# Attention inside an attention, expert and feed-forward kernel: maxima nine steps ahead of the scores instead of ten, the splits of v one step later

## The chip, the core and the metric

One core of a Trainium2 chip runs the whole program. TensorE (PE; its weight loads PEld) multiplies, VectorE (DVE), ScalarE (ACT) and GpSimd (POOL) do the element work, and SyncE (SP) issues nearly all transfers, in the order of the program. The metric is the device time of one execution in microseconds (us). Before the change the median of three runs is 687.61 us (685.89 to 688.62).

## The reference, cut to what matters

```python
# attention: q, k, v are (2, 8, 768, 64); proj is (64, 6)
q_bits = einsum(q, proj) > 0 ; k_bits = einsum(k, proj) > 0
q_bucket = sum(q_bits * 2**i) ; k_bucket = sum(k_bits * 2**i)
scores = where(q_bucket == k_bucket, 1/8 * q @ k.T, -1e9)
scores = scores - max(scores)            # over the keys
attn = exp(scores) / (sum(exp(scores)) + 1e-9)
x = (attn @ v) as (1536, 512)
# router and experts: 8 experts, each token goes to one of them
logits = x @ w_gate + modality_bias[modality_id]
e = argmax(logits) ; gate = softmax(logits)[e]
x = gate * (relu(x @ w1[e]) @ w2[e])
# feed-forward
h = x @ w_in
out = (max(h, 0) + alpha * min(h, 0)) @ w_out
```

Queries and keys match where all six signs of their projections agree. The kernel computes this match as matrix products of rows of signs (the hash), so that the mask comes out of the same multiplication as the scores.

## The kernel before

The program runs the attention first (to about 242 us), then the experts, then the feed-forward layers. The change touches the attention alone, with the router operations that are laid between its steps. There are 16 heads and 96 steps: step s computes the scores of head s // 6 for the key block s % 6 against all 768 queries.

The loop over s (L950 to L975) writes the work of a step in the order of a string of letters (ORDER), and every engine runs its instructions in the order in which they are written. A step holds:

- a and b: ST, the scores of two halves of 384 queries, two matmuls each (L861, L862), and ScalarE's exponential (L863). The matmul L861 reads rows of the head's operand tile `op`: its signs and, in row 96, the row `mr`, minus the maxima of the queries.
- m and n: MAX, the products of signs (L829) for a key block u that lies some steps ahead, and VectorE's maxima over them (L830). How far ahead is set by LA: u stays below s + 6 + LA + 1. The tuple cap limits how many blocks the first steps take.
- e: the 16-bit copy of the exponentials and what it leaves (L867 on ScalarE, L868 on GpSimd).
- p: POSTa, the maxima of a head put together when its sixth block is done (L832). One step later, at the step's end, POSTb transposes them on TensorE (L835), VectorE makes the row from that (L837), and SyncE writes it into the operand tile (L838); two flag rows (L841, L842) follow a step later.
- A: AV, the products with v (L876 to L878) of two steps at a time, in odd steps.
- N: NORM, the normalisation of a head that is done (L888 to L890).
- V and o: the work that the table PLAN sets to a step: vsplit, ScalarE's scaling of a head's v (L755, in V) and VectorE's split in two parts (L759, L760, in o).
- L, last in the step: what PLAN sets there, in the order in which it was registered: T (the split of a head's q and k: L711, L712, and five transfers of operand rows, L650), Z (the hash matmuls L802 to L804 of a half of 384 columns, VectorE's comparison L809, and four transfers of hash rows), vtot (12 small matmuls with v's sums, L766 to L769), vscale and vscale2 (L734 to L749), POSTb.
- D: the transfers that the step before put off: hash rows first, then operand rows and flag rows, then loads of later heads (L656, L657).

Score and maxima products share five PSUM tiles, and everything small that TensorE writes shares two, called misc. After each step the function hook runs: the router's constants, transpositions and logits of x, and the router's first lumps (the list first: each entry is the step in which the generator goes one lump further). The lumps that the change moves are the token positions (L346 to L353), the one-hot table (L357, L274) and the gates (L233 to L239). In steps 80 and 81 the hook issues the first expert's weight loads (L630).

PLAN's entries for a group are added to its first step: sp gives the step of vsplit of each of four heads in a period of 24 steps, tot how many steps later its vtot runs, Z3 the steps of head 3's two hash halves.

Of the kernel before, what the change touches and what calls it, by code (L numbers as in the profile page):

```python
# [22 lines left out]
G = 2  # L23
NP = 5
NH = 16
LA = 4
MO3 = "HMTh"
STEPS = 13.0
DELAY = 0.7
# [8 lines left out]
ORDER = "aVDNmbnefopAL"  # L38
PM = 2
PLAN = dict(  # L40
    v0=(1, 3, 4), T3=(2, 2), Z3=(4, 5), T=(2, 4, 5, 7), Z=(8, 10), ld=0, am1=(4, 6, 8, 9), am=(4, 6, 8,
    10), sc=(13, 15), tot=3, tot0=6, sp=(-2, 4, 10, 18), cap=(3, 2, 0, 1), x=(1, 2, 7, 3), x3=(0, 1, 2, 2), x4=(9, 10, 13, 11), w1=(91, 92, 95, 96, 97, 98, 99, 100), ga=(87, 88, 90), vl=1, am0=(0, 0), Z2=(0, 1), x6=(0, 1, 6, 4), first=(57, 58, 59, 60, 66, 72, 75, 78, 83, 84, 85, 86),
)
NPRE = 3
NT = 22
# [458 lines left out]
def _program(base, tc, nc, q, k, v, proj, mod, w_gate, mbias, w1, w2, win, wout, alpha, out):  # L504
# [445 lines left out]
    for s in range(96+LAG+2):  # L950
        us=[u for u in range(nu,min(96,s+6+LA+1,nu+(PLAN["cap"][s] if s<len(PLAN["cap"]) else 2)))]; nu+=len(us)
        fs=dq[:]; dq.clear()
# [615 lines left out]
```

## Time and profile before

| | |
|---|---|
| median of three runs | 687.61 us |
| profiled execution, as a run | 686.88 us |
| its span, first to last instruction | 685.1 us |
| PE busy | 656.4 us (96%) |
| PEld busy | 556.2 us (81%) |
| DVE busy | 446.7 us (65%) |
| ACT busy | 315.3 us (46%) |
| POOL busy | 236.0 us (34%) |
| mean granted TensorE clock | 0.987 of 2.4 GHz |

The span is one execution; the 1.8 us that it lacks to the run's time lie around it. A busy TensorE counts overlapping matmuls as one stretch, so a share of 96% does not say that nothing waits: a wait shows as an idle time before an instruction, with what ended it. The attention is where other engines are busy too; the last 443 us are long chains of matmuls.

### The profile page before, as it was taken

What the parts mean: (1) busy time and instruction counts of PE and PEld (TensorE: products, weight loads), DVE (VectorE), ACT (ScalarE), POOL (GpSimd) and SP (SyncE); (2) the same over time, 40 slices, a digit from 0 to 9 for tenths busy, and PEclk for the clock granted to TensorE, in tenths of its full rate; (3) what the DMA queues carried; (4) which work ended last, traced back from release to release, by engine and by line L of the source; (5) the groups of instructions that cost most, each with busy time, mean ns of one, the idle gap of its engine ahead of it and who ended that gap; (6) DMA issues with size and microseconds to landing.
All of it is one profiled execution on the core that took longest, in us unless ns stands there. A gap on an engine that the chain in (4) does not pass through costs nothing.

```text
span 685.1 us, 12778 instructions
## 1 busy us (share of the span) xinstructions
PE 656.4 (96%) x4938; PEld 556.2 (81%) x4938; DVE 446.7 (65%) x927; ACT 315.3 (46%) x536; POOL 236.0 (34%) x211
## 2 busy tenths in 40 slices
PE   7789999999999988999999999999999999999995
PEld 6578898998788878898888987888888888888884
DVE  6887878788888778455735668999443444433332
ACT  5567788887787843033423256665211111111111
POOL 8767999987967501310000202040030000200002
PEclk9979999999999999999999999999999999999998
DMA  8466864866603139385320834441020000100001
GB/s 217 129 146 142 187 154 97 185 185 138 140 11 125 49 107 395 119 321 201 108 61 11 285 120 154 131 146 62 1 93 1 15 16 0 47 16 0 1 0 61
DMA packets 32859, 75.02 MB, mean 110 GB/s; under 512 B 7276, under 2 KB 7366, under 8 KB 32534
## 3 DMA queue, kind: packets, MB, share of 16 engines
q1 hardware_dynamic: 29700, 64.43, 33.0%
q0 software_dynamic: 2960, 9.70, 4.3%
q8 instruction: 39, 0.64, 0.4%
q14 instruction: 30, 0.25, 0.1%
q10 hardware_dynamic: 130, 0.00, 0.0%
HBM read 49.79 MB, written 14.68 MB: 94 GB/s over the span
## 4 chain that ended last, share of the span: by engine, by line
PE 54%; DVE 1%; ACT 1%; issue 1%; POOL 1%; ACTq 0%; POOLq 0%
PE o L1413 19%; PE h L1387 18%; PE y L1074 8%; PE g L1054 8%; PE tr L1257 1%; POOL out_dram L1430 1%; PE tr L1041 0%; DVE w L1232 0%; DVE op L1232 0%; ACT op L1230 0%; DVE gl L620 0%; ACT gf L1391 0%; ACT q L1392 0%; ACT w L1230 0%; DVE big L1197 0%
## 5 line engine op out<-in xcount | busy, mean ns | idle before, releaser
L868 POOL TENSOR_TENSOR El<-E,Eh 128x768 f16<-128x768 f32 x87 | 142.7, 1652 | 36.6 <-ACT Eh L867 22.7
L863 ACT ACTIVATE E<-st 128x384 f32<-128x384 f32 x192 | 89.2, 494 | 53.3 <-PE st L862 49.8
L830 DVE TENSOR_REDUCE mx<-mxp 128x1 f32<-128x384 f32 x192 | 97.6, 548 | 9.2 <-PE mxp L829 8.7
L617 ACT ACTIVATE gh<-gf 128x512 fp32r<-128x512 f32 x48 | 30.3, 631 | 142.7 <-PE o L1413 132.2
L867 ACT ACTIVATE Eh<-E 128x768 f16<-128x768 f32 x94 | 79.8, 849 | 0.0
L861 PE MATMUL st<-op 97*128 97x384 f32 x192 | 72.9, 380 | 1.6 <-DMA op<-mr 1.3
L829 PE MATMUL mxp<-op 76*128 76x384 f32 x192 | 65.9, 357 | 7.3 <-ACT E L863 2.5
L620 DVE TENSOR_TENSOR gl<-gf,gh 128x512 fp32r<-128x512 f32 x48 | 33.1, 690 | 59.2 <-ACT gh L617 57.2
L1430 POOL DMA_INDIRECT out_dram<-x,did x12 | 11.8, 984 | 167.8 <-DVE x L1427 89.1
L1387 PE MATMUL h<-big,op 128*128 128x512 f32 x256 | 67.9, 393 | 0.0
L862 PE MATMUL st<-op 128*128 128x384 f32 x192 | 65.8, 343 | 0.0
L1413 PE MATMUL o<-op,gh 128*128 128x512 f32 x192 | 64.2, 395 | 0.0
L1245 POOL DMA_INDIRECT yg<-ys,dpos x10 | 12.3, 1231 | 138.3 <-DVE x L1197 72.8
L876 PE MATMUL av<-vh,Eh 128*128 128x65 f16 x576 | 58.5, 196 | 1.3 <-DVE big L890 1.3
L876 PEld LDWEIGHTS <-Eh 128*128 128x128 f16 x576 | 52.5, 98 | 8.4 <-issue 6.2
L1074 PE MATMUL y<-op,hh 128*128 128x512 f32 x172 | 58.6, 399 | 0.0
L877 PE MATMUL av<-vl,Eh 128*128 128x64 f16 x576 | 58.0, 194 | 0.0
L878 PE MATMUL av<-vh,El 128*128 128x65 f16 x576 | 57.8, 195 | 0.0
L1387 PEld LDWEIGHTS h<-big,op 128*128 128x128 f32 x256 | 48.1, 188 | 10.9
L877 PEld LDWEIGHTS <-Eh 128*128 128x128 f16 x576 | 53.2, 99 | 0.0
L878 PEld LDWEIGHTS <-El 128*128 128x128 f16 x576 | 53.1, 98 | 0.0
L1395 DVE TENSOR_SCALAR gf<-h,al 128x512 f32<-128x512 f32 x33 | 24.8, 751 | 41.7 <-PE h L1387 41.7
(424 smaller groups left out, 1483.2 us busy)
## 6 DMA issues: line engine op xcount, KB each, us to landing
r<-in_moe_w_dram SPq DMA_DIRECT2D x14, 1024.0 KB
op<-B SPq DMA_DIRECT2D x32, 192.0 KB
op<-A SPq DMA_DIRECT2D x28, 192.0 KB
op<-A SPq DMA_DIRECT2D x13, 384.0 KB
ys<-zero SPq DMA_DIRECT2D x19, 256.0 KB
op<-in_moe_w_in_dram SPq DMA_DIRECT2D x4, 1024.0 KB
op<-in_moe_w_out_dram SPq DMA_DIRECT2D x4, 1024.0 KB
ys<-ysb SPq DMA_DIRECT2D x13, 256.0 KB
```

The costliest lines, as they stand in the source:

```text
L829: mm(p[:,0:384],t[0:76,2,c*128:(c+1)*128],t[0:76,1,a*384:a*384+384],start=True,stop=True)
L830: nc.vector.tensor_reduce(out=mx[h][:,c,a:a+1],in_=p[:,0:384],axis=AX.X,op=ALU.max)
L861: mm(p[:,0:384],t[0:97,1,js],t[0:97,2,qs],start=True,stop=False)
L863: nc.scalar.activation(E[s][0][:,qs],p[:,0:384],AF.Exp,scale=0.125)
L867: else: nc.scalar.activation(eh,e,AF.Copy)
L868: (nc.vector if s>=ELD else nc.gpsimd).tensor_tensor(out=el,in0=e,in1=eh,op=ALU.subtract)
L876: mm(a[:,c*65:c*65+65],eh[:,cs],VH[h//4%2][:,j,h%4,:],start=(j==0 and c==0),stop=False,skip_group_check=True)
L877: mm(a[:,c*65:c*65+64],eh[:,cs],VL[h//4%2][:,j,h%4,:],start=False,stop=False,skip_group_check=True)
L878: mm(a[:,c*65:c*65+65],el[:,cs],VH[h//4%2][:,j,h%4,:],start=False,stop=False,skip_group_check=True)
L1074: nc.tensor.matmul(yps[key][i], a[:, ts], w[:, c], start=(c == 0 and m == 0), stop=(c == 7 and m == 2))
L1387: nc.tensor.matmul(p, terms[t][0][:, kk, cs], terms[t][1][:, kk], start=(n == 0), stop=(n == 11))
L1413: nc.tensor.matmul(po[b][i], a[:, ts], w[:, c % 2], start=(c == 0 and n == 0), stop=(c == 15 and n == 2))
```

## The change

Six entries of the tables change. No instruction is added or taken away; the order changes.

```diff
-LA = 4
+LA = 3
 ...
-    Z3=(4, 5), ... tot=3, ... sp=(-2, 4, 10, 18), cap=(3, 2, 0, 1),
+    Z3=(5, 5), ... tot=2, ... sp=(-1, 5, 11, 17), cap=(3, 2, 0, 1, 0),
 ...
-    first=(57, 58, 59, 60, 66, 72, 75, 78, 83, 84, 85, 86),
+    first=(57, 58, 59, 60, 66, 72, 78, 80, 81, 84, 85, 86),
```

With LA = 3 a step's maxima are those of the block nine steps on instead of ten, and so POSTa and POSTb of a head come one step later: POSTb of head h moves from the end of step 6h - 4 to the end of step 6h - 3. Head 1's stay in steps 3 and 4, since the limits of the first four steps are the same. Step 4 has no maxima. The splits of three heads of four come a step later and of the fourth a step earlier, all now in the step behind a NORM; vtot of the three stays, of the fourth it comes two steps earlier. Head 3's first hash half moves from step 4 to step 5, and the router's lumps move: positions from step 75 to 78, one-hot table from 78 to 80, gates from 83 to 81.

On TensorE, head 5's transposition L835 stood at the end of an even step, behind two score pairs and two maxima (op_143 is head 4's operand tile, whose scores these are; mt_182 the maxima of odd heads):

```order
 L861 MATMUL st<-op_143 128x384
 L862 MATMUL st<-op_143 128x384
-L829 MATMUL mxp<-op_140 128x384
+L829 MATMUL mxp<-op_139 128x384
 L861 MATMUL st<-op_143 128x384
 L862 MATMUL st<-op_143 128x384
-L829 MATMUL mxp<-op_140 128x384
-L835 MATMUL misc<-ident,mt_182 6x128
+L829 MATMUL mxp<-op_139 128x384
```

It now stands behind the odd step's products with v (av; the last two are the flag rows fl and v's sums vt):

```order
 L882 LDWEIGHTS fl_187
 L882 MATMUL av<-vt,fl_187 128x65
+L835 MATMUL misc<-ident,mt_182 6x128
 L861 MATMUL st<-op_143 128x384
 L862 MATMUL st<-op_143 128x384
```

So L835 moved behind the 36 products of two steps, and the maxima of the step are those of the block before.

On SyncE the order around it stays. This is the queue from head 5's row (op_139) to head 6's (op_140), the same before and now; A and B are the two parts of the q and k of heads 8 and 9, big_74 holds the loaded q and k:

```order
66 L838 DMA op_139<-mr 1x6x128
67 L842 DMA fl_189<-ft 1x6x128 x2
68 L650 DMA op_142<-A 64x2x768
69 L650 DMA op_142<-A 64x768 x2
70 L650 DMA op_142<-B 64x768 x2
...
76 L656 DMA big_74<-in_k_dram 64x768
77 L657 DMA big_74<-in_q_dram 64x768
78 L838 DMA op_140<-mr 1x6x128
```

Nothing moved in this piece; what changed is when its first row's data is made.

On VectorE, at the end of the piece around a NORM (L888 to L890; am are v's magnitudes, big_74 the hash rows, vh and vl the split of v):

```order
 L889 RECIPROCAL r<-r 128x6
 L890 TENSOR_TENSOR big_72<-av,r 128x6x64
+L830 TENSOR_REDUCE mx<-mxp 128x1 x2
+L731 TENSOR_REDUCE am<-vr 128x1
+L809 TENSOR_SCALAR big_74<-misc,tv 48x384
 L830 TENSOR_REDUCE mx<-mxp 128x1 x2
 L759 CAST vh_191<-misc 128x6x64
 L760 TENSOR_TENSOR vl_193<-misc,vh_191 128x6x64
-L731 TENSOR_REDUCE am<-vr 128x1
-L809 TENSOR_SCALAR big_74<-misc,tv 48x384
-L830 TENSOR_REDUCE mx<-mxp 128x1 x2
```

The split moved behind the hash comparison and two more maxima, away from the normalisation.

## Rows read from the trace of the kernel before

**Rows 1.** Windows: us, busy time of each engine (instructions), TensorE's clock, DMA share, GB/s.

```profile
32.20:42.40 10.20, 8.56 (x51) 6.79 (x51) 7.43 (x18) 4.80 (x9) 7.15 (x5) 0.50 0.53 121
94.00:109.50 15.50, 15.50 (x194) 13.72 (x193) 13.89 (x34) 12.75 (x25) 15.50 (x16) 1.00 0.93 203
```

**Rows 2.** Timeline of TensorE, steps 3 to 15: start, us, instruction, [idle before, its releaser].

```profile
31.98 0.40 PE L747 MATMUL misc<-dg,one 128*128 128x4 f32 x2 [1.54 <-DVE dg L743]
33.88 0.66 PE L829 MATMUL mxp<-op 76*128 76x384 f32 x1 [0.66 <-ACT E L863]
38.08 0.37 PE L835 MATMUL misc<-ident,mt 128*6 128x128 f32 x1 [0.98 <-DVE vl L760]
48.28 0.41 PE L829 MATMUL mxp<-op 76*128 76x384 f32 x1 [0.83 <-ACT A L711]
...
52.80 0.34 PE L861 MATMUL st<-op 97*128 97x384 f32 x1
63.09 0.41 PE L829 MATMUL mxp<-op 76*128 76x384 f32 x1 [1.26 <-DMA op<-big]
64.33 0.34 PE L829 MATMUL mxp<-op 76*128 76x384 f32 x1
```

**Rows 3.** Timeline of SyncE's queue, rows of heads 2 to 9 and their neighbours.

```profile
51.89 0.77 SPq L838 DMA_DIRECT2D op<-mr  x1
65.50 0.77 SPq L838 DMA_DIRECT2D op<-mr  x1
66.32 0.43 SPq L76 DMA_DIRECT2D mi<-in_moe_modality_id_dram  x1
80.61 0.76 SPq L838 DMA_DIRECT2D op<-mr  x1
91.65 0.72 SPq L838 DMA_DIRECT2D op<-mr  x1
118.62 0.71 SPq L838 DMA_DIRECT2D op<-mr  x1
144.07 0.92 SPq L838 DMA_DIRECT2D op<-mr  x1
146.94 0.35 SPq L892 DMA_DIRECT2D x_d<-big  x1
```

**Rows 4.** Timeline of TensorE, first score matmuls of steps and one transposition.

```profile
66.77 0.43 PE L861 MATMUL st<-op 97*128 97x384 f32 x1
85.85 0.45 PE L861 MATMUL st<-op 97*128 97x384 f32 x1 [0.71 <-DMA op<-mr]
90.69 0.27 PE L835 MATMUL misc<-ident,mt 128*6 128x128 f32 x1
93.34 0.44 PE L861 MATMUL st<-op 97*128 97x384 f32 x1
111.83 0.42 PE L861 MATMUL st<-op 97*128 97x384 f32 x1
120.00 0.42 PE L861 MATMUL st<-op 97*128 97x384 f32 x1
138.28 0.43 PE L861 MATMUL st<-op 97*128 97x384 f32 x1
145.76 0.44 PE L861 MATMUL st<-op 97*128 97x384 f32 x1
165.77 0.41 PE L861 MATMUL st<-op 97*128 97x384 f32 x1 [0.54 <-DMA op<-mr]
```

**Rows 5.** DMA busy tenths in 40 slices of 80.5:85.5, 105:110 and 132:137.

```profile
DMA  9999899989995999989999999969788280100010
DMA  9696996989959693969899799998949597592010
DMA  7989989999998979995997999999995969772201
```

**Rows 6.** Waits of TensorE from 166 to 225: us in total, times, longest.

```profile
PE mxp L829 <- ACT E L863: 1.4, 3, 0.5
```

More of the change, by code (lines that the diff above doesn't have):

```diff
@@ L40 @@
 PLAN = dict(
-    v0=(1, 3, 4), T3=(2, 2), Z3=(4, 5), T=(2, 4, 5, 7), Z=(8, 10), ld=0, am1=(4, 6, 8, 9), am=(4, 6, 8,
-    10), sc=(13, 15), tot=3, tot0=6, sp=(-2, 4, 10, 18), cap=(3, 2, 0, 1), x=(1, 2, 7, 3), x3=(0, 1, 2, 2), x4=(9, 10, 13, 11), w1=(91, 92, 95, 96, 97, 98, 99, 100), ga=(87, 88, 90), vl=1, am0=(0, 0), Z2=(0, 1), x6=(0, 1, 6, 4), first=(57, 58, 59, 60, 66, 72, 75, 78, 83, 84, 85, 86),
+    v0=(1, 3, 4), T3=(2, 2), Z3=(5, 5), T=(2, 4, 5, 7), Z=(8, 10), ld=0, am1=(4, 6, 8, 9), am=(4, 6, 8,
+    10), sc=(13, 15), tot=2, tot0=6, sp=(-1, 5, 11, 17), cap=(3, 2, 0, 1, 0), x=(1, 2, 7, 3), x3=(0, 1, 2, 2), x4=(9, 10, 13, 11), w1=(91, 92, 95, 96, 97, 98, 99, 100), ga=(87, 88, 90), vl=1, am0=(0, 0), Z2=(0, 1), x6=(0, 1, 6, 4), first=(57, 58, 59, 60, 66, 72, 78, 80, 81, 84, 85, 86),
 )
```

## The prediction, before the run

> **What bounds the kernel now.** I read the page first: TensorE is busy nearly the whole span, and the chain of waits is TensorE work almost alone, so an edit that changes no instruction, as this one, can only move stretches in which TensorE waits. Next I read the windows, to see where the clock is not full, and then TensorE's timeline through the attention (22 to 242 us): 96 steps, each two score pairs (L861, L862) and two maxima (L829), an odd step with the value products L876 to L878 of two steps at its end. The reader is to see three kinds of wait in it.
>
> First, the start. TensorE waits 1.54 us until 31.98, then runs at half clock from 32.2 to 42.4, with waits of 0.66 us (a maximum of head 2), 0.98 us (the transposition L835 of head 1, for a misc buffer that head 0's v split holds) and 0.83 us (head 3's first maximum) in steps 4 to 8 [rows 1, 2]. Second, hashes: 1.26 us until 63.09, when head 4's first maximum has its hash rows [rows 2]. Third, the maxima's row mr, which the first score pair of a head multiplies with: the pairs of heads 4 and 10 wait 0.71 and 0.54 us for it [rows 4].
>
> Then I read SyncE's queue, which explains the third. Every transfer of the attention is issued there in order. After an odd head's mr come its two flag rows, the five operand rows of one head, two loads, the same for another head, two loads, and only then the next even head's mr. From head 5's mr at 91.65 [rows 3] to 109.5 us the queues move data at a DMA share of 0.93 [rows 1]; the digits of the DMA view stay at 9 or near it until about 109.4 us, and for head 8's row until 136.4 [rows 5]. So an even head's row cannot land before the data ahead of it has, and all that data stands behind the odd head's row, whose issue TensorE's own progress sets. That loop (odd step, odd mr, 15 us of transfers, even mr, even head's first pair) is what I price.
>
> **The change, part by part.** Times are sums against the profiled execution (686.88 us with its edges, 685.1 us of span); the median of the runs shown is 687.61, 0.73 above it, and I put the sum on that.
>
> *Steps 4 to 8.* Step 4 has no maxima now and head 3's first hash half goes to step 5. The 0.66 goes, since that maximum runs a step later. The 0.98 goes, since no hash half takes a misc buffer between the v split and L835, which now gets the other one. The 0.83 goes, since head 3's first maximum runs in step 9. That is 2.47 us. A pair of maxima not yet done at this place is worth another 0.35 (two matmuls that overlap, of 0.34 to 0.41 each [rows 2]), which is paid back when the maxima end. The 1.54 stands ahead of everything that moves and stays, and so does the fall of the clock behind it. Whether the half clock ends sooner no row shows: at its earliest a third of the 10.2 us goes, worth about 1.5 us (an estimate: half of 3.4, less the waits in it); or new waits for score buffers take back 1.2 (four maxima fewer in step 4 are four more behind the split on VectorE). I take 3.0 for the gain by step 9, between 1.5 and 4.5.
>
> *Head 4's hash.* Its four issues stand behind head 2's mr, head 5's operands and two flag rows. From that mr's issue at 51.89 [rows 3] to the maximum at 63.09 [rows 2] are 11.2 us of queue. In the changed kernel the mr leaves 0.96 us (the distance of L835 at 90.69 [rows 4] and its issue at 91.65 [rows 3]) after the end of step 9, not of step 8: at 52.80 + 0.96, so the hash is there at 64.96, less the gain. The maximum that needs it stands a step later, where 64.33 is now [rows 2]. So the wait does not go although it has a step more: 0.63 of the gain is lost there.
>
> *Head 4's mr row.* Head 3's row was issued at 65.50 [rows 3], and 20.35 us later, at 85.85 [rows 4], head 4's first pair began. Now head 3's row is ready 0.96 after the end of step 15, 66.77 + 0.96 = 67.73, less the gain so far; one router issue of 0.43 (mi) goes ahead of it instead of behind [rows 3], so 67.73 + 19.9 = 87.6 less the gain: 1.7 lost, and TensorE waits some 2.4 us there instead of 0.71. Of the 3.0 so far 0.7 is left. Bounds: 2.2 gained to 0.8 lost, as the start turns out.
>
> *Heads 6, 8 and 10.* L835 of every head moves from the end of an even step to the end of the odd step behind it, which holds the value products: for head 5 from 90.69 to 93.34 [rows 4]. The pair that needs the row does not move. For odd heads I take no wait, since no data stands ahead of their rows in the queue; the rows of before, where none of them waits, bound this at a few tenths each, 2 us in all. For the even ones the loop counts:
> - Head 6: head 5's row goes 2.65 us later (94.3 against 91.65), and the data with it. The DMA digits fall at 84.7 and the pair of head 4 starts 1.15 us later [rows 4, 5]; by the same 1.15 head 6's row is there at 110.55, with 1.3 us to spare against the pair at 111.83. New wait 1.35, or 1.0 if a hole of 0.4 us in the queue closes. I take 1.2.
> - Head 8: head 7's row goes at 120.00 + 0.96, not 118.62: 2.33 later. To spare: 138.28 less 137.55, or 0.7. New wait 1.6 (1.3 to 2.2).
> - Head 10: 145.76 + 0.96 = 146.7 against 144.07, 2.65 later, of which 0.4 was idle ahead of the write of x_d at 146.94 (the row and two flag rows end there at 146.5). Nothing to spare: the pair at 165.77 waits already [rows 3, 4]. New wait 2.3 on top (2.2 to 2.65).
>
> Together 5.1. Nothing hides it: TensorE is in order, and the score pair has everything of its head behind it. Head 12 has spare time, because heads 14 and 15 have no loads behind theirs, and head 14's row, which now stands behind the first weight load of 1 MB, does not wait for it: that load has nothing left to wait for and is issued some 10 us earlier.
>
> The ring order is also what the Trainium skill says: in "DMA: Bandwidth & Descriptors", section on queues, rings and completion order, each DMA engine takes descriptors in the order of the ring. The same page puts the fixed cost of a DMA near 2.0 us (section on the anatomy of one DMA, fitted on the GpSimd path). By that price alone a row would be there 2 us after its issue whatever stands ahead, and heads 6 and 8 would not wait (the second rival's case). The trace is against it where it shows: head 4's row was issued at 80.61 [rows 3], and its pair waited until 85.85 [rows 4].
>
> *v's splits, lumps.* The splits leave the even step with the normalisation for the odd one behind it, the totals keep their place, and the router's small operations leave step 75, where VectorE ran them straight ahead of a normalisation and a split. Three waits of up to 0.5 us for score buffers that ScalarE had not emptied, 1.4 us in all, stand between 166 and 225 [rows 6], two of them behind such pile-ups; the moved lumps may make a new one. I take 1.0 gained (0 to 2, with the small stalls under the view's limit).
>
> Sum: 3.0 gained, 0.6 + 1.7 + 5.1 lost, 1.0 gained, 0.35 paid back: +3.75. From 687.61 that is 691.4 us.
>
> **The rivals.**
> - *The clock falls behind the new waits.* The wait that ended at 31.98 was 1.54 us, and half clock followed; the 1.26 us at 63.09 was not followed by it [rows 1, 2]. The new waits at heads 4 and 10 are 2.4 and 2.8. Each fall costs half of its length: with a third of the stretch seen, 1.5 us or more. Against it: TensorE is dense on both sides. One or two falls: 693 to 695.
> - *The even rows are not late.* The change does not do what I say because the queue has air in it, or the data drains faster when it starts on idle engines. Then of the 5.1 about 1.2 is left (head 10): 0.7 + 1.0 gained, 1.55 lost, no change: 687.4. For it: TensorE showed no wait at heads 6 and 8. Against: the share of 0.93.
> - *Faster: only waits go.* The half clock ends a third sooner (4.5 gained by step 9), the hash is in time, no row is late, and the pile-ups go (2.0): up to 6.5, so 681 to 684. It decides where the mr rows have over 3 us to spare, which the two waits at heads 4 and 10 speak against.
>
> **How the numbers follow.** 0.5% is 3.4 us, about what a measurement of this kernel can tell from no change: below 684.2 is faster, above 691.05 slower. The forecast has 0.55, with 689.0 to 693.5 as its own range, some 0.32 of it above the bound; the clock 0.15, all slower; the rows in time 0.17, all the same; only waits go 0.13, faster. That makes slower 0.47, the same 0.40, faster 0.13. The range of 684.5 to 695 leaves out most of the last case and a second fall of the clock.
>
> **What would show it.** Right: TensorE's waits at L861 for mr at heads 4, 6, 8 and 10 of about 2.4, 1.2, 1.6 and 2.8 us; L838 of odd heads some 2.5 us closer to their pair; L835 of head 1 without a wait. Wrong: pairs of heads 6 and 8 that start without a wait; or a half-clock stretch gone or much shorter, or one that is new. If the waits come as I say and the time falls, the gain at the start was larger than TensorE's row there let me see.

## The result and the profile after

The changed kernel takes 692.26 us (median of 5 runs, 690.3 to 694.35), against 687.43 for the kernel before beside it: ratio 1.0071, 95% interval 1.0045 to 1.0098, slower by 4.8 us. A second set on another occasion gave 692.16 us, ratio 1.0105 (1.0079 to 1.0131). The forecast was 691.4. The profiled execution took 691.76 us, its span is 690.0 against 685.1.

TensorE's timeline of the changed kernel, steps 3 to 15 (start, us, instruction, [idle before, its releaser]), answers to [rows 2]:

```profile
30.57 0.59 PE L747 MATMUL misc<-dg,one 128*128 128x4 f32 x2 [1.54 <-DVE dg L743]
32.45 0.41 PE L835 MATMUL misc<-ident,mt 128*6 128x128 f32 x1
35.32 0.69 PE L829 MATMUL mxp<-op 76*128 76x384 f32 x1 [0.22 <-ACT E L863]
61.75 0.42 PE L829 MATMUL mxp<-op 76*128 76x384 f32 x1 [2.09 <-DMA op<-big]
```

The 1.54 stands; L835 of head 1 waits for nothing; of the waits of 0.66, 0.98 and 0.83 us one of 0.22 is left. The wait for head 4's hash has grown from 1.26 to 2.09. The first score pairs of heads 4, 6, 8 and 10 in the same timeline, which answer to [rows 4]:

```profile
85.16 0.69 PE L861 MATMUL st<-op 97*128 97x384 f32 x1 [2.27 <-DMA op<-mr]
...
115.05 0.44 PE L861 MATMUL st<-op 97*128 97x384 f32 x1 [0.88 <-DMA op<-mr]
...
143.29 0.45 PE L861 MATMUL st<-op 97*128 97x384 f32 x1 [1.40 <-DMA op<-mr]
...
172.25 0.45 PE L861 MATMUL st<-op 97*128 97x384 f32 x1 [0.73 <-DMA op<-mr]
```

Four pairs wait for the row mr where two did, 5.3 us instead of 1.3. Two windows (columns as in [rows 1]), first the start's half-clock stretch, then what follows head 4's wait:

```profile
30.40:40.70 10.30, 9.91 (x61) 8.19 (x62) 6.43 (x16) 4.94 (x10) 8.47 (x6) 0.50 0.67 160
...
85.10:91.80 6.70, 6.64 (x60) 6.34 (x61) 2.23 (x4) 3.32 (x6) 3.17 (x3) 0.50 0.42 128
```

The first is the old one, as long as before. The second is new: TensorE is granted 1.2 GHz and not 2.4 from about the end of the 2.27 us wait on. SyncE's queue from head 3's row to head 4's and beyond, which answers to [rows 3], and VectorE's making of head 4's row:

```profile
64.87 0.78 SPq L838 DMA_DIRECT2D op<-mr  x1
65.69 0.47 SPq L76 DMA_DIRECT2D mi<-in_moe_modality_id_dram  x1
66.29 1.46 SPq L842 DMA_DIRECT2D fl<-ft  x2
67.86 2.90 SPq L650 DMA_DIRECT2D op<-A  x3
70.86 1.36 SPq L650 DMA_DIRECT2D op<-B  x2
72.27 0.60 SPq L656 DMA_DIRECT2D big<-in_k_dram  x1
72.92 0.60 SPq L657 DMA_DIRECT2D big<-in_q_dram  x1
73.62 3.37 SPq L650 DMA_DIRECT2D op<-A  x3
77.09 1.43 SPq L650 DMA_DIRECT2D op<-B  x2
78.56 0.60 SPq L656 DMA_DIRECT2D big<-in_k_dram  x1
79.21 0.59 SPq L657 DMA_DIRECT2D big<-in_q_dram  x1
79.90 0.75 SPq L838 DMA_DIRECT2D op<-mr  x1
```

```profile
78.02 0.28 DVE L837 TENSOR_SCALAR mr<-misc 6x128 fp32r<-6x128 f32 x1 [1.03 <-PE misc L835]
```

The queue issues without a gap of a microsecond for 15 us. Head 4's row is made at 78.30, is issued at 79.90, and its last packet lands at 84.12; TensorE, done with step 23 at 82.89, gets on at 85.16. The DMA digits from the row's issue on, which answer to [rows 5], stay at 9 or near it until shortly before it lands:

```profile
DMA  8979496979989989597999969932118432016431
```

TensorE's waits for ScalarE over the same steps (60 to 87, here 172.3 to 230 us), which answer to [rows 6], are 0.8 us against 1.4:

```profile
PE mxp L829 <- ACT E L863: 0.8, 2, 0.5
```

Where the time went, from the starts of each step's first score matmul in the two profiled executions (changed minus before, us):

| stretch | from | to | change | what stands there |
|---|---|---|---|---|
| to step 3 | 0 | -1.40 | -1.40 | nothing that moved: before had 3.4 us of half clock at 11.7 |
| to step 9 | -1.40 | -3.81 | -2.41 | the waits that went |
| to step 14 | -3.81 | -3.21 | +0.60 | step 9 (0.50): L835 of head 2 now stands there, and short stops |
| to step 16 | -3.21 | -2.48 | +0.73 | head 4's hash |
| to step 24 | -2.48 | -0.69 | +1.79 | head 4's row |
| to step 26 | -0.69 | +2.27 | +2.96 | the new half-clock stretch |
| to step 36 | +2.27 | +3.22 | +0.95 | head 6's row |
| to step 48 | +3.22 | +5.01 | +1.79 | head 8's row |
| to step 60 | +5.01 | +6.47 | +1.46 | head 10's row, and small waits before it |
| to the end | +6.47 | +4.88 | -1.59 | fewer waits for score buffers in steps 68 to 78 |

### The profile page after: what moved, and what is told of

Its sections match the earlier page's. It is cut to its first block, busy times and chain, and to the rows that moved or that the text cites. A ratio compares the mean times of both kernels' runs of the same rounds, so it can differ in the third digit from the quotient of the medians.

```text
span 690.0 us, 12782 instructions
## 1 busy us (share of the span) xinstructions
PE 657.6 (95%) x4938; PEld 558.2 (81%) x4938; DVE 445.9 (65%) x927; ACT 315.5 (46%) x536; POOL 236.5 (34%) x211
## 4 chain that ended last, share of the span: by engine, by line
PE 54%; DVE 1%; ACT 1%; issue 1%; POOL 1%; ACTq 0%; POOLq 0%
PE o L1413 19%; PE h L1387 18%; PE y L1074 8%; PE g L1054 8%; PE tr L1257 1%; POOL out_dram L1430 1%; PE tr L1041 0%; DVE w L1232 0%; DVE op L1232 0%; ACT op L1230 0%; DVE gl L620 0%; ACT gf L1391 0%; ACT q L1392 0%; ACT w L1230 0%; DVE big L1197 0%
## 5 line engine op out<-in xcount | busy, mean ns | idle before, releaser
L868 POOL TENSOR_TENSOR El<-E,Eh 128x768 f16<-128x768 f32 x87 | 142.9, 1652 | 40.8 <-ACT Eh L867 19.9
```

The costliest lines, as they stand in the source:

```text
L868: (nc.vector if s>=ELD else nc.gpsimd).tensor_tensor(out=el,in0=e,in1=eh,op=ALU.subtract)
```

## The experiments

Each is compared with runs of the kernel before beside it (medians 686.37, 685.78 and 685.30 in the three sets), so ratios are the measure.

**The parts alone.** First the start.

```diff
-    Z3=(4, 5), ... cap=(3, 2, 0, 1),
+    Z3=(5, 5), ... cap=(3, 2, 0, 1, 0),      # on the kernel before
```

> The kernel before with the fifth limit of the maxima (0) and head 3's first hash half in step 5; still ten steps ahead, splits and lumps as before. Theory (the late rows of the maxima made the changed kernel slower; the start alone gains): the waits of 0.66, 0.98 and 0.83 us go, some 2.4 us are gained by step 9 and kept to the end, since head 2's row leaves as early as before: about 685.0 us, TensorE's wait for head 4's hash rows stays near 1.3 us, the rows of heads 4 and 10 are waited for by 0.5 to 0.8 us each. Rival (the start is paid back where the next resource is late): the gain is gone by step 16, 687.4 us.

684.33 us, ratio 0.9973 (0.9955 to 0.9991): 2.0 us gained, and in the profile what is gained by step 16 is kept to the end. Head 4's hash is waited for by 0.3 us, and not by the 1.3 expected. TensorE's waits for mr there:

```profile
PE st L861 <- DMA op<-mr: 0.7, 2, 0.4
```

Next the distance alone.

```diff
-LA = 4
+LA = 3      # on the kernel before
```

> The kernel before with nothing but the maxima nine steps ahead instead of ten. Theory: the waits for mr of the changed kernel come back here (2.3 us at head 4, 0.9, 1.4 and 0.7 or more at heads 6, 8, 10) and so does the half-clock stretch behind head 4's, and nothing is gained at the start: 687.4 + 7 = about 694 us (692 to 697). Rival (the splits or lumps that moved are what made it slower): within 1 us of before, 687.4.

697.2 us, ratio 1.0164 (1.0144 to 1.0185): 10.8 us lost, just beyond the expected range. The waits for the row are there, the half clock behind head 4's too, and beyond them a hash half that waits 1.8 us for a normalisation (L802) and a second wait of 0.5 us for hash rows, near the start:

```profile
PE st L861 <- DMA op<-mr: 4.8, 3, 2.2
PE mxp L829 <- DMA op<-big: 2.5, 2, 2.0
...
PE misc L802 <- DVE r L888: 1.8, 1, 1.8
```

```profile
85.20:91.90 6.70, 6.02 (x49) 5.75 (x50) 2.23 (x4) 3.31 (x6) 2.63 (x4) 0.50 0.49 136
```

Then the splits and lumps.

```diff
-    tot=3, ... sp=(-2, 4, 10, 18), ... first=(..., 72, 75, 78, 83, 84, 85, 86)
+    tot=2, ... sp=(-1, 5, 11, 17), ... first=(..., 72, 78, 80, 81, 84, 85, 86)      # on the kernel before
```

> The kernel before with nothing but v's splits, their totals and the router's lumps moved. Theory: 1 us gained (0 to 2) by fewer waits for score buffers behind a normalisation: about 686.4 us. Rival (the new places bring waits of the router's transpositions for VectorE's normalisation, 0.9 and 0.5 us in the changed kernel): 688.5 us.

684.58 us, ratio 0.9970 (0.9955 to 0.9984): 1.8 us gained. The three parts sum to +7.0 us; the whole gave +4.8 and +6.9. So they act side by side as far as these runs can tell, and nine steps are the only part that costs.

**The place of L835.** The change made the row late by a step; here half of a step is given back.

```diff
 ...
-   if u%6==5: POSTa(u//6); sl_at(s+PB,lambda h=u//6:POSTb(h))
+   if u%6==5: POSTa(u//6); post_at(s+PB,lambda h=u//6:POSTb(h))
 ...
+   if o==("L" if s<7 else "b"):      # behind the step's second score pair
+       for f in post.get(s,[]): f()
```

> The changed kernel with one instruction group put elsewhere: the transposition of the maxima L835 with its row and flags stands behind the second score pair of the odd step, ahead of its last maxima and of the value products, from head 2 on; so the odd heads' rows leave some 1.6 us earlier. Theory: the waits for mr at heads 4, 6, 8 and 10 (2.27, 0.88, 1.40 and 0.74 us) fall to 0.7 or less, the half-clock stretch behind head 4's wait goes (3 us), head 4's hash wait falls by 0.8 or more: 692.3 - 7 = about 685.5 us. Rival 1 (a row needs its number of steps, not its place within one): no change, 692. Rival 2 (L835 now waits for VectorE's maxima, 0.5 us at each of 14 heads): waits at L835 of 7 us in all, no gain.

685.56 us, ratio 0.9993 (0.9979 to 1.0008): nearly all of the loss is gone with nine steps still. Waits from 50 to 245 us:

```profile
PE misc L835 <- DVE mt L832: 3.0, 3, 1.1
...
PE st L861 <- DMA op<-mr: 0.7, 1, 0.7
```

Only head 10's pair still waits (0.7), none of these waits is for head 4's hash, and the second rival is there in part: L835 waits 3 us for VectorE's maxima. No stretch of the attention runs at half clock, but not even the start does, which the edit leaves alone: this execution (683.85 us, mean clock 0.997) is the fastest of twelve, and the others have 0.985 to 0.994. How much of the 6.7 us below the changed kernel comes from the clock is not shown.

**Without the nine steps.**

```diff
-LA = 3
+LA = 4      # on the changed kernel; the limits, Z3, tot, sp and first stay
```

> The changed kernel with the maxima ten steps ahead again; its start (limits, hash half of head 3), its splits and its lumps kept. Theory (the nine steps are the only part that costs; the two others gained 2.0 and 1.8 us alone, in different stretches): 686.4 - 3.8 = about 682.6 us. Rival (the parts share one gain): 684.5 us.

681.76 us, ratio 0.9946 (0.9928 to 0.9965). This beats both kernels, by 4.0 and by some 10 us.

**Eleven steps ahead.**

```diff
-LA = 4
+LA = 5      # on the kernel of 681.76 us
```

> The kernel before with the start, splits and lumps of the changed one and the maxima eleven steps ahead. Theory (the rows have time enough at ten, and the hash rows get a step less): the waits for mr go to zero (1 us gained), but the hash of head 4 is waited for by some 3.5 us instead of 1.3, and those of later even heads by up to 2 us each: 682.6 - 1 + 2.2 + (0 to 6), about 685 us (683.5 to 690). Rival (the further ahead the better): 680 to 681 us.

693.95 us, ratio 1.0133 (1.0107 to 1.0159), beyond the expected range. The direction was right, the size was not. Waits from 55 to 245 us:

```profile
PE mxp L829 <- DMA op<-big: 3.1, 3, 1.6
PE misc L196 <- DVE vt L769: 2.1, 3, 1.0
PE misc L835 <- DVE vt L769: 1.6, 3, 0.5
```

The hash waits come, at fewer heads and shorter than expected (1.6 us for head 4, not 3.5). What was not expected: L835 now stands in the steps that make v's sums, right behind them, and it (heads 3, 7 and 11) and the router's L196 behind it wait for VectorE's vt. And one thing moves that the expectation left out: a row that is made a step earlier stands on SyncE ahead of the second head's five transfers, with one batch between the two rows and not two. This is head 4's row with what follows it:

```profile
77.08 0.76 SPq L838 DMA_DIRECT2D op<-mr  x1
77.96 2.83 SPq L650 DMA_DIRECT2D op<-A  x3
```

So this run changes the queue's order together with the distance, and it does not say which of the two the hash waits come from. Of the three distances tried ten steps are the best, with late rows at nine and hash rows and v's sums at eleven.

**Is it SyncE's queue, or the data?** Even heads' rows on a queue of their own:

```diff
-        nc.sync.dma_start(out=f32(OP[h%NP][96:97,2, ...
+        (nc.gpsimd if h%2==0 else nc.sync).dma_start(out=f32(OP[h%NP][96:97,2, ...
```

> The changed kernel; only the rows mr of the even heads 2 to 14 are issued by GpSimd instead of SyncE, at the same place of the program. Theory (an even head's row is late because SyncE's queue holds 15 us of data ahead of it): the rows land before their pairs, the waits at heads 4, 6, 8 and 10 (5.3 us in all) and the half-clock stretch behind head 4's (3 us) go: 692.3 - 7 = about 685 us. Rival 1 (too few steps between the transposition and the pair, whatever the queue): the waits stay, 692. Rival 2 (the DMA engines are the bound, not SyncE's order): the row waits on GpSimd's queue as well, half of the waits stay, 689.

702.8 us, ratio 1.0250 (1.0229 to 1.0271), slower than the theory and both rivals had it. The theory as I had put it falls. GpSimd's queue with head 4's row, TensorE's first pair of head 4, and the row's instructions as one line of the source (who waited; DMA to landing):

```profile
84.49 1.66 POOL L868 TENSOR_TENSOR El<-E,Eh 128x768 f16<-128x768 f32 x1
86.08 0.54 POOL L838 DMA_DIRECT2D op<-mr  x1
```

```profile
91.57 0.44 PE L861 MATMUL st<-op 97*128 97x384 f32 x1 [2.05 <-DMA op<-mr]
```

```profile
  PE st L861: 9.7, 6
...
DMA to landing us min/median/max: 1.6/4.9/5.8
```

The row, free of SyncE's order, takes as long: its last packet lands 4.1 us after the issue, against 4.2 from SyncE (the landing of the view comes later, when the semaphore tells of it). It also leaves late, behind GpSimd's own work (L868 of 1.66 us), at head 2 for the first time with a wait of 3.8 us. That GpSimd's way is slow in itself is a rival that the same trace answers: head 14's row, issued by GpSimd at 231.88 with hardly any data under way, has its last packet after 1.2 us. The two windows, columns as in [rows 1], DMA share last but one (it counts packets by their start, so it can pass 1):

```profile
86.09:90.20 4.11, 3.43 (x52) 3.08 (x50) 3.62 (x8) 2.77 (x5) 3.84 (x6) 1.00 1.01 215
231.90:233.20 1.30, 0.81 (x5) 0.35 (x5) 1.20 (x6) 1.30 (x4) 1.18 (x3) 1.00 0.03 5
```

**Less data ahead of the row.**

```diff
     def OD(h,ns=range(5)):
+        if h>4: ns=range(3)
```

> The changed kernel without the two transfers of part B for heads 5 to 15 (384 of 960 KB of each head; the scores lack that correction), all else in place. Theory (data ahead of the row): rows of heads 6 to 10 land in 2 to 2.5 us, their waits (0.9, 1.4, 0.7 us) go, head 4's falls below 1 us and with it the half-clock stretch (3 us), head 4's hash wait falls by 1.5 us: about 684.5 us (682.5 to 687). Rival 1 (too few steps, not data): 692. Rival 2 (the order of SyncE alone, not the bytes: its issues get 3 us shorter for two heads, the data only drain sooner): the hold of 1.4 to 2.0 us between the row's making and its issue goes, the landing time stays over 3 us.

683.55 us, ratio 0.9965 (0.9950 to 0.9980). No pair waits for a row. VectorE makes head 4's row, SyncE issues it at once, and TensorE does not stop (lines are one higher here):

```profile
76.38 0.28 DVE L838 TENSOR_SCALAR mr<-misc 6x128 fp32r<-6x128 f32 x1 [1.03 <-PE misc L836]
```

```profile
76.68 0.75 SPq L839 DMA_DIRECT2D op<-mr  x1
```

```profile
81.10 0.42 PE L862 MATMUL st<-op 97*128 97x384 f32 x1
```

Its last packet lands 1.75 us after the issue (4.22 in the changed kernel); those of heads 6, 8 and 10 after 1.47, 1.94 and 2.59. So both rivals fall: the steps are enough, and with the hold the landing time goes too. Fewer transfers are also fewer issues on SyncE; that the data count and not only the issues is what head 4's row on GpSimd shows.

**The data behind the row.**

```diff
-    T=(2, 4, 5, 7),
+    T=(2, 4, 5, 9),
```

> The changed kernel; the five operand transfers of every second head (5, 7, 9, ...) and that head's loads are issued two steps later, so that the even head's row mr stands ahead of them on SyncE instead of behind them. Maxima still nine steps ahead, L835 where the change put it. Theory (the even row is late because of the data ahead of it, whatever queue it is on): the rows land in 1.5 to 2.5 us instead of 3 to 4.2 and are not held on SyncE, the waits for mr at heads 4 to 10 (5.3 us) fall below 1 us, the half-clock stretch at 85 us goes, and head 4's hash rows, ahead of head 5's operands now, come in time (2.1 us): about 683 us (681.5 to 686). Rival (four and a half steps are too short for a row even on an empty queue): waits stay, 690 to 692 us.

696.74 us, ratio 1.0169 (1.0143 to 1.0196), far from what was expected. The rows do what was expected: none of heads 4 to 10 is held, they land in 1.5 to 1.8 us, their pairs do not wait (head 3's pair does, by 0.96 us). The time goes the other way, since the next maxima wait now, for the hash rows behind the data that was moved, or for ScalarE (why that is late at 119 us is open):

```profile
89.83 0.41 PE L829 MATMUL mxp<-op 76*128 76x384 f32 x1 [2.12 <-DMA op<-big]
...
119.45 0.41 PE L829 MATMUL mxp<-op 76*128 76x384 f32 x1 [1.93 <-ACT E L863]
...
150.11 0.41 PE L829 MATMUL mxp<-op 76*128 76x384 f32 x1 [1.67 <-DMA op<-big]
```

```profile
90.40:93.60 3.20, 3.20 (x47) 2.71 (x45) 1.00 (x2) 1.22 (x2) 3.20 (x3) 0.50 0.79 255
121.10:127.70 6.60, 6.60 (x54) 6.10 (x52) 3.91 (x11) 3.92 (x8) 3.97 (x3) 0.50 0.11 24
151.80:155.00 3.20, 3.20 (x27) 2.85 (x24) 1.71 (x6) 1.01 (x3) 2.54 (x2) 0.50 0.89 215
```

The three windows are granted 1.2 GHz, each begins within two microseconds of such a wait's end. Late rows were exchanged for late hash rows. The same edit on the fastest kernel:

```diff
-    T=(2, 4, 5, 7),
+    T=(2, 4, 5, 8),      # on the kernel of 681.76 us
```

> The fastest kernel so far (start, splits and lumps of the change, maxima ten steps ahead; 681.8 us) with the same reordering: the even head's row ahead of the second head's operand transfers, which go one step later. Theory: its waits of 0.2 and 0.8 us at heads 4 and 10 and a wait of the maxima behind the hash go, 1 us: about 681 us (680 to 682). Rival (the rows were in time, and what is put behind them is late instead: hash rows for the next maxima): 683 to 686 us.

688.44 us, ratio 1.0049 (1.0030 to 1.0067): a miss, and the rival's mechanism at more than its price. Waits for hash rows from 50 us on, where the fastest kernel has none over 0.2:

```profile
PE mxp L829 <- DMA op<-big: 3.1, 3, 1.6
```

**The half clock behind the wait.**

```diff
+        if s==24:
+            p=misc()
+            for _ in range(8): mm(p[:,128:256],one,one,start=True,stop=True)
```

> The changed kernel with eight matmuls of 128 columns on constants (some 2.1 us, their result is not read) ahead of the first score pair of head 4, where TensorE waited 2.27 us for mr. Theory (the half-clock stretch of 85.0 to 91.9 us follows from TensorE having stood still before it): the pair starts at the same time, the wait for mr there is under 0.3 us, the stretch goes and 3 us are gained: about 689.3 us. Rival (the clock falls by something else than the wait): the stretch stays, 692.3 us or up to 1 us more.

In the profile it came as expected, with no wait and full clock behind it:

```profile
84.21 2.02 PE L955 MATMUL misc<-one 128*128 128x128 f32 x16 [0.18 <-DVE vl L760]
86.11 0.45 PE L861 MATMUL st<-op 97*128 97x384 f32 x1
```

```profile
85.00:92.00 7.00, 7.00 (x84) 6.63 (x82) 3.92 (x10) 4.69 (x9) 3.87 (x5) 1.00 0.47 131
```

From step 24 to 26 nothing is lost against before, where the changed kernel lost 2.96 us. But the time did not fall: 692.06 us, ratio 1.0095 (1.0073 to 1.0116). To compare:

> The changed kernel once more, beside the others on the same chip, to compare with the kernel whose wait at head 4 was filled with matmuls. Theory: ratio to before 1.007, the wait of some 2.3 us at head 4 and the half-clock stretch right behind it come again. Rival (that stretch was one execution's): no stretch, the span is some 3 us shorter than 690.0.

Ratio 1.0105, as told above, and wait and stretch came again:

```profile
85.37 0.69 PE L861 MATMUL st<-op 97*128 97x384 f32 x1 [2.23 <-DMA op<-mr]
```

```profile
84.50:91.10 6.60, 5.73 (x43) 5.42 (x44) 2.23 (x4) 3.32 (x6) 2.51 (x5) 0.50 0.50 137
```

So the stretch came with the wait in all three profiles in which head 4's pair waits over 2 us for a row from SyncE (these two and the nine steps alone), and filling the wait took it away in one. What it costs over many runs stays open: three runs of the filled kernel took 690.7 to 691.1 us at a mean clock of 0.987 to 0.989, three 693.0 to 693.4 at 0.980 to 0.982. The changed kernel's eleven runs spread over the same clocks (0.980 to 0.991), so the filled wait did not lift them; where the clock fell in the runs without a profile is not known.

The two profiles of the changed kernel show how much one execution differs from the next. The second has no half clock at the start (the first has 10.2 us of it) and is 5.1 us ahead of before at step 9, not 3.8. But there the wait for head 4's hash was followed by 3.4 us of half clock, where the first has none:

```profile
60.45 0.65 PE L829 MATMUL mxp<-op 76*128 76x384 f32 x1 [2.11 <-DMA op<-big]
```

At step 16 the two are level (2.2 and 2.5 us ahead), and the spans are 690.1 and 690.0.

**One number for the mechanism.** From the issue of an odd head's row to the last packet of the next even head's row (us, from the traces):

| kernel | 3 to 4 | 5 to 6 | 7 to 8 | 9 to 10 |
|---|---|---|---|---|
| before | 19.6 | 17.9 | 17.8 | 20.7 |
| changed | 19.3 | 17.8 | 18.8 | 20.2 |
| start alone | 19.6 | 18.1 | 17.9 | 20.7 |
| nine steps alone | 19.2 | 18.0 | 18.5 | 20.3 |
| L835 earlier | 19.3 | 17.9 | 17.9 | 20.4 |
| even rows by GpSimd | 18.7 | 18.0 | 17.6 | 19.7 |
| less data | 15.2 | 14.9 | 15.4 | 17.0 |
| second batch behind the row | 13.9 | 14.9 | 17.0 | 16.1 |
| eleven steps | 13.2 | 13.4 | 13.2 | 16.2 |

As long as both batches stand between the two rows, it hardly moves with the step, the place of L835 or the queue. It drops by 3 to 4 us when two of each head's five transfers are left out, and by 2 to 6 when the second batch stands behind the even row. In these last three kernels an even row is issued as soon as it is made but for one (head 10's at eleven steps), so there the number says when the row was made, and the row could have come sooner still. The even row comes when the data between the two rows has drained.

## Why the prediction was right

The time was forecast within 0.9 us, for the reason given, and with errors in the sum that cancelled: that it came so close is luck. By the prediction's own list the four waits and L835 of head 1 are signs of being right (odd rows came 1.7 to 2.2 us closer to their pairs, 2.5 forecast), and the new half-clock stretch is one of being wrong.

- *Steps 4 to 8*, 3.0 gained: 2.4 by step 9 in the profile, of which 0.6 is lost again by step 14, ahead of the hash; 2.0 alone. The half clock of the start kept its length, 10.2 us, in this profile.
- *Head 4's hash*, 0.63 lost, the wait stays: 0.73 from step 14 to 16, wait 2.09. The step of the sum is right to a hundredth: from the issue of head 2's row to the end of the wait are 11.2 us before (51.89 to 63.09) and now (50.55 to 61.75).
- *Head 4's row*, 1.7 lost, wait 2.4: 1.79 and 2.27.
- *Heads 6, 8 and 10*, 1.2, 1.6 and 2.3 lost: 0.95, 1.79 and 1.46. Head 10's own wait was 0.73, not 2.8, since 0.3 to 0.6 us each of small waits in steps 52 to 59 came first and gave its row time. Odd heads and heads 12 and 14 did not wait, as said; in the second profile, without half clock at the start, head 1's pair waited 1.4.
- *The loop*, odd row, data, even row: shown, by the table and by the kernel with less data. The part of the step that fails is its carrier. I had put it on SyncE's order; GpSimd's queue did not help, so what counts is the data that is under way when the row is issued. The hold on SyncE (1.6 us for head 4) is only part of it. With nothing ahead a row needs 1.4 to 1.5 us to its last packet on SyncE, and 1.6 to its landing on GpSimd at the least; behind data 3.0 to 4.2 to the last packet. A fixed cost of near 2.0 us for a DMA on GpSimd's path (the Trainium skill, "DMA: Bandwidth & Descriptors", on the anatomy of one DMA) is somewhat above the first and well below the second.
- *Splits and lumps*, 1.0 gained (0 to 2): 1.8 alone.
- *The clock behind a new wait*, priced as a rival at 0.15 and left out of the sum: it came at head 4, 2.96 us in the profile. This is the largest error, and the start fell short by another 1.2 (0.6 by step 9, 0.6 by step 14). Against them stand head 10 (0.8 less than forecast), the end (0.9 better, with the 0.35 that was not seen to be paid back), and a start of the profiled execution that was 1.4 us ahead before anything had moved. Whether the median holds those 3 us is what the filled kernel left open.

The rival in which the rows are not late had 0.17; the four waits speak against it. That only waits go (0.13) was right for two of the three parts: without the nine steps they give 681.8 us, inside the 681 to 684 that it named.

## What to carry to other kernels

Before a producer of a small transfer is moved, measure the time from the last transfer issued before the large ones to the landing of the small one: where it is constant, the small one cannot come sooner, and a step taken from it comes back as a wait. Here, putting it ahead of the data moved the lateness to what stood behind, another queue did not help, and less data or an earlier start of the whole batch took it away. See also whether a step more or less changes the order of the queue, as it did at eleven. Time the parts of a mixed change one by one: here two gained 2 us each and the third lost 11.

## What the runs showed of the hardware

- A row of 3 KB needs 1.4 to 1.5 us from its issue on SyncE to its last packet when little or no data is under way (odd heads from 3 on in the changed kernel), 3.0 to 4.2 behind the operand rows (heads 4 to 10 there). Through GpSimd's queue it is 4.1 us for head 4 at a DMA share of 1.01 and 1.2 us for head 14 at 0.03.
- The granted clock fell to 1.2 GHz with single waits of TensorE of 1.3 to 2.3 us in an otherwise dense stretch (longest: 3.8), for 3.4 or 6.8 us. It did not always: of the 19 waits of 1.5 us or more between 50 and 240 us in the fourteen profiles, half clock began during 12 or within 2 us behind them. The 2.09 us wait at 61.75 of the changed kernel was not followed by it; the same wait in its second profile, 2.11 us at 60.45, was.
- Executions of one kernel differ in where the clock falls: the two profiles of the changed kernel have 10.2 us and nothing at the start, nothing and 3.4 us at 60.5, and both have 6.8 us at head 4's row.
